# Causal blocks with carried sums of k^T v, transposes on VectorE and double PSUM banks in a retention-plus-SwiGLU kernel

## The chip, the core and the metric

One core of a Trainium2 chip runs the whole program. The metric is the device time of one execution in microseconds, as the median of the runs. The TensorE clock has two levels, 1.2 and 2.4 GHz; the profile gives the granted clock as a share of 2.4 GHz.

## The reference

Retention attention without softmax over 8 sequences of 576 tokens and 8 heads of 64, then RMS norm and a SwiGLU block over the 4608 tokens. All is float32, but the three weight matrices arrive as float64.

```python
scores = scale * np.matmul(q, k.transpose(0, 1, 3, 2))
Dmat = np.where(rel >= 0, gamma[:, None, None] ** rel[None, :, :], 0.0)   # rel = query - key
x = np.matmul(scores * Dmat, v)            # then (B,H,S,D) -> (B*S, H*D)
xn = x / np.sqrt(np.mean(x * x, axis=-1, keepdims=True) + 1e-06) * rms_g
g = xn @ w_gate
out = (g * (1.0 / (1.0 + np.exp(-g))) * (xn @ w_val)) @ w_out
```

## The kernel before

Two streams of work share TensorE. A **job** of attention is one sequence and one pair of heads, 32 jobs in all, and its result is one 128-row chunk of x, transposed (features on the partitions, tokens on the free axis). A **unit** of the FFN is 384 tokens, 12 units in all, and up to four units of x are on chip.

A job: `load` brings q, k and v of both heads by DMA on SP's queue. `turn` transposes q and k with TensorE (tiles tp_q and tp_k, three products of 96 tokens each) and ScalarE copies them out of PSUM as qT and kT. `scores` takes one tile of 128 keys and one block of queries: two products (s, one for each head, in the upper and lower 64 rows of the array), and VectorE multiplies each by a table of decays, which also holds the causal zeros, into ret. Every pair of key tile and block of queries that isn't wholly in the future is computed. `values` multiplies ret by v (the heads side by side in 64 columns of the array each) and sums over the key tiles in PSUM (av); ScalarE copies the sum to x. `attention_step` issues the scores of one tile, then the values of the tile before it, so s and av take turns on TensorE.

When a unit of x is whole, `norm_1` squares it on ScalarE (sq), sums over the features with 12 products of one column (ms), takes the power -1/2 on GpSimd (r) and puts it on diagonals; `norm_2` spreads it over the partitions with one product (rb), and VectorE scales x. Then `gate` and `value` (12 column blocks each, four products of 384 columns per block), Silu on ScalarE, the product h on VectorE, and `contract` (three times 12 products of 512 columns).

The order is written by hand. The loop at the end of the program gives TensorE a step of attention, or a step of the FFN when the FFN's columns fall behind attention's share (it starts 17% behind), or when attention would need a fifth unit of x.

The weights come as float64 in 36 chunks of 128 x 512. `round_chunk` turns one into float32 with six VectorE instructions and one of ScalarE; `weights_to` rounds up to a chunk number and asks for later loads on ScalarE's queue. After the first 8 steps of attention one chunk is rounded with every second step, and `gate` and `contract` round what they need and a little more. PSUM is three pools of single banks: 3 for s, 2 for tp and av, 3 for the FFN.

A float32 product shows in the profile as two records for TensorE and two for its weight loads.

Of the kernel before, what the change touches and what calls it, by code (L numbers as in the profile page):

```python
# [17 lines left out]
def _decay_table(H, S, D):  # L18
    """T[p, h, c] = gamma_h ** (c - p) / sqrt(D) where c >= p, else 0: a key tile that begins at
    token t uses column q - t for query q."""  # L20
    gamma = 1.0 - 2.0 ** (-5.0 - np.arange(H, dtype=np.float64))
    rel = np.arange(S)[None, :] - np.arange(P)[:, None]
    t = np.where(rel >= 0, gamma[:, None, None] ** np.maximum(rel, 0)[None], 0.0) / np.sqrt(D)
    return np.ascontiguousarray(t.transpose(1, 0, 2)).astype(np.float32)


@with_exitstack
def kernel(
# [15 lines left out]
    NHP = H // 2  # head pairs, which are also the 128-row chunks of d_model  # L44
    NF = DFF // P
    NKT = -(-S // P)  # key tiles; the last one is short
    JT = 6  # token tiles of a loaded q or k
    PT = S // JT
# [4 lines left out]
    assert (D, DM, NHP * P) == (64, H * D, DM) and S % JT == 0 and NTOK % U == 0  # L53
# [8 lines left out]
    ps_s = ctx.enter_context(tc.tile_pool(name="ps_s", bufs=3, space=PS))  # L62
    ps_m = ctx.enter_context(tc.tile_pool(name="ps_m", bufs=2, space=PS))
    ps_f = ctx.enter_context(tc.tile_pool(name="ps_f", bufs=3, space=PS))
# [6 lines left out]
    decay = const.tile([P, H, S], F32, name="decay")  # L71
# [10 lines left out]

    def load(j):
        b, hp = jobs[j]
        hs = slice(2 * hp, 2 * hp + 2)
        for nm, src in (("q", q), ("k", k)):
            t = raw.tile([PT, JT, 2, D], F32, tag=nm + "raw", name=f"{nm}raw_{j}")
            for e in range(2):
                nc.sync.dma_start(
                    out=t[:, :, e], in_=src[b, 2 * hp + e].rearrange("(j p) d -> p j d", p=PT)  # L90
                )
            st[j][nm + "raw"] = t
        t = raw.tile([P, 2, NKT, D], F32, tag="v", name=f"v_{j}", bufs=3)
        full = S // P
        for e in range(2):
            nc.sync.dma_start(
                out=t[:, e, :full],
                in_=v[b, 2 * hp + e, : full * P].rearrange("(c p) d -> p c d", p=P),
            )
        if S % P:  # L100
            nc.sync.dma_start(
                out=t[: S % P, :, full], in_=v[b, hs, full * P :].rearrange("h p d -> p h d")
            )
        st[j]["v"] = t

    def turn(j, nm):
        """q or k of a head pair with (head, d) on the partitions."""
        d = st[j]
        t = att.tile([P, S], F32, tag=nm + "T", name=f"{nm}T_{j}")
        tv = t.rearrange("p (j t) -> p j t", j=JT)  # L110
        half = JT // 2
        for n in range(2):
            tp = ps_m.tile([P, half, PT], F32, tag="m", name=f"tp_{nm}_{j}_{n}")
            for i in range(half):
                nc.tensor.transpose(  # L115
                    out=tp[:, i], in_=d[nm + "raw"][:, n * half + i], identity=ident[:PT, :PT]
                )
            nc.scalar.copy(out=tv[:, n * half : (n + 1) * half], in_=tp)  # L118
        d[nm + "T"] = t

    def blocks(b):
        """The queries of a sequence, cut where the FFN's units are."""
        cuts = [0] + [c - b * S for c in range(0, NTOK, U) if 0 < c - b * S < S] + [S]
        return list(zip(cuts[:-1], cuts[1:]))

    def tiles(j):
        return [
            (j, q0, q1, kt)
            for q0, q1 in blocks(jobs[j][0])
            for kt in range(NKT)  # L130
            if kt * P < q1
        ]

    def scores(j, q0, q1, kt):
# [3 lines left out]
        k0, k1 = kt * P, min(kt * P + P, S)  # L138
        lo, n = max(q0, k0), k1 - k0
        w = q1 - lo  # L140
        ret = att.tile([P, 2, U], F32, tag="ret", name=f"ret_{j}_{q0}_{kt}", bufs=3)
        ss = [ps_s.tile([P, 512], F32, tag="s", name=f"s_{j}_{q0}_{kt}_{e}") for e in range(2)]
        for e in range(2):
            r = slice(e * D, e * D + D)
            nc.tensor.matmul(  # L145
                ss[e][:n, :w], lhsT=d["kT"][r, k0:k1], rhs=d["qT"][r, lo:q1], start=True, stop=True
            )
        for e in range(2):
            nc.vector.tensor_tensor(  # L149
                out=ret[:n, e, :w], in0=ss[e][:n, :w],  # L150
                in1=decay[:n, 2 * hp + e, lo - k0 : q1 - k0], op=ALU.mult,
            )
        d["ret", q0, kt] = ret
# [127 lines left out]
    def attention_step(n, t):  # L281
# [4 lines left out]
        if j + 1 < len(jobs):  # L286
            if n == 2:
                turn(j + 1, "q")
# [145 lines left out]
```

## Time and profile before

| | us |
|---|---|
| median of 3 runs (1737.16 to 1738.85) | 1737.68 |
| span of the profiled execution, first to last instruction | 1732.1 |
| TensorE busy | 1609.2 |
| VectorE busy | 387.0 |
| ScalarE busy | 213.7 |
| GpSimd busy | 10.9 |
| mean granted clock, share of 2.4 GHz | 0.917 |

The profile of the execution gives its span; an execution's own time contains what lies around the span too, and for the median that is 5.6 us. Busy time is the union of an engine's records, and a busy TensorE need not be at its peak: records overlap, and at half the clock the same product is busy twice as long. A stretch is read with the granted clock beside it.

### The profile page before, as it was taken

What the parts mean: (1) busy time and instruction counts of PE and PEld (TensorE: products, weight loads), DVE (VectorE), ACT (ScalarE), POOL (GpSimd) and SP (SyncE); (2) the same over time, 40 slices, a digit from 0 to 9 for tenths busy, and PEclk for the clock granted to TensorE, in tenths of its full rate; (3) what the DMA queues carried; (4) which work ended last, traced back from release to release, by engine and by line L of the source; (5) the groups of instructions that cost most, each with busy time, mean ns of one, the idle gap of its engine ahead of it and who ended that gap; (6) DMA issues with size and microseconds to landing.
All of it is one profiled execution on the core that took longest, in us unless ns stands there. A gap on an engine that the chain in (4) does not pass through costs nothing.

```text
span 1732.1 us, 14109 instructions
## 1 busy us (share of the span) xinstructions
PE 1609.2 (93%) x5784; PEld 842.0 (49%) x5784; DVE 387.0 (22%) x940; ACT 213.7 (12%) x422; POOL 10.9 (1%) x18
## 2 busy tenths in 40 slices
PE   5778976999999999999999899999999899999899
PEld 2334532554454554554554554454554554455454
DVE  2655375121111111211111211310111310410110
ACT  1112121110011110110110100110110100200000
POOL 0000000000000000000000000000000000000000
PEclk9556976999998999998999899899899899989899
DMA  6333232100100100100000101200101200100000
GB/s 180 100 88 89 60 113 80 27 14 13 33 14 20 31 17 20 47 0 20 26 21 19 41 1 28 59 0 13 27 7 32 56 1 0 46 1 6 12 0 18
DMA packets 134927, 59.89 MB, mean 35 GB/s; under 512 B 115920, under 2 KB 128208, under 8 KB 134864
## 3 DMA queue, kind: packets, MB, share of 16 engines
q1 hardware_dynamic: 119360, 37.77, 8.7%
q10 hardware_dynamic: 15504, 21.24, 3.9%
q8 instruction: 45, 0.74, 0.2%
q14 instruction: 18, 0.15, 0.0%
HBM read 49.55 MB, written 9.44 MB: 34 GB/s over the span
## 4 chain that ended last, share of the span: by engine, by line
PE 88%; DVE 6%; ACT 4%; issue 1%; DMA 1%; POOLq 0%; SPq 0%; ACTq 0%; DVEq 0%
PE gate L218 23%; PE out L241 22%; PE val L218 22%; PE s L145 8%; PE av L165 7%; PE ms L188 3%; PE tp_k L115 2%; PE tp_q L115 1%; ACT exp L338 1%; DVE exp L342 1%; ACT sq L185 1%; ACT kT L118 1%; PE rb L206 1%; DVE exp L339 1%; ACT x L173 1%
## 5 line engine op out<-in xcount | busy, mean ns | idle before, releaser
L241 PE MATMUL out<-w_out,h 128*128 128x512 f32 x864 | 402.8, 619 | 23.4 <-DVE w_out L352 23.4
L218 PE MATMUL gate<-x,w_gate 128*128 128x384 f32 x1152 | 411.9, 502 | 5.8 <-DVE x L210 5.8
L218 PE MATMUL val<-x,w_val 128*128 128x384 f32 x1152 | 397.8, 488 | 0.0
L218 PEld LDWEIGHTS gate<-x,w_gate 128*128 128x128 f32 x1152 | 221.7, 195 | 168.3 <-issue 15.9
L218 PEld LDWEIGHTS val<-x,w_val 128*128 128x128 f32 x1152 | 216.6, 190 | 151.4 <-issue 5.8
L241 PEld LDWEIGHTS out<-w_out,h 128*128 128x128 f32 x864 | 165.3, 197 | 232.6 <-issue 191.2
L149 DVE TENSOR_TENSOR ret<-s,decay 128x384 f32<-128x384 f32 (+4 forms) x480 | 160.2, 374 | 527.3 <-PE s L145 526.0
L233 DVE TENSOR_TENSOR h<-silu,val 128x384 f32<-128x384 f32 x144 | 79.8, 554 | 612.4 <-PE val L218 612.1
L145 PE MATMUL s<-qT,kT 64*128 64x384 f32 (+4 forms) x960 | 189.9, 433 | 23.5 <-DVE ret L149 23.3
L145 PEld LDWEIGHTS s<-qT,kT 64*128 64x128 f32 (+1 forms) x960 | 88.2, 198 | 146.9 <-issue 109.5
L228 ACT ACTIVATE silu<-gate 128x384 f32<-128x384 f32 x144 | 70.7, 491 | 697.7 <-PE gate L218 686.7
L165 PE MATMUL av<-ret,v 128*64 128x384 f32 (+4 forms) x960 | 156.2, 407 | 0.0
L165 PEld LDWEIGHTS av<-ret,v 128*64 128x64 f32 (+1 forms) x960 | 51.3, 146 | 74.9 <-issue 61.1
L188 PE MATMUL ms<-mean_w,sq 128*128 128x1 f32 x288 | 55.5, 325 | 26.9 <-ACT sq L185 26.9
L188 PEld LDWEIGHTS ms<-mean_w,sq 128*128 128x128 f32 x288 | 54.4, 293 | 29.1 <-ACT sq L185 29.1
L247 ACT COPY o<-out 128x512 f32<-128x512 f32 x36 | 21.1, 586 | 341.7 <-PE out L241 341.7
L115 PE MATMUL tp_k<-ident,kraw 96*128 96x96 f32 x192 | 33.5, 291 | 19.4 <-ACT kT L118 15.5
L115 PE MATMUL tp_q<-ident,qraw 96*128 96x96 f32 x192 | 32.6, 291 | 18.3 <-DMA qraw<-in_q_dram 9.7
L173 ACT COPY x<-av 128x384 f32<-128x384 f32 (+1 forms) x64 | 25.5, 399 | 177.4 <-PE av L165 153.4
L118 ACT COPY kT<-tp_k 128x288 f32<-128x288 f32 x64 | 25.5, 399 | 129.0 <-PE tp_k L115 128.9
L115 PEld LDWEIGHTS tp_k<-ident,kraw 96*128 96x128 f32 x192 | 20.5, 156 | 41.4 <-ACT kT L118 21.9
L115 PEld LDWEIGHTS tp_q<-ident,qraw 96*128 96x128 f32 x192 | 21.1, 160 | 32.1 <-issue 15.7
(33 smaller groups left out, 261.4 us busy)
## 6 DMA issues: line engine op xcount, KB each, us to landing
qraw<-in_q_dram SPq DMA_DIRECT2D x64, 144.0 KB, 2.5
kraw<-in_k_dram SPq DMA_DIRECT2D x64, 144.0 KB, 2.5
out_dram<-o SPq DMA_DIRECT2D x36, 256.0 KB, 2.1
v<-in_v_dram SPq DMA_DIRECT2D x64, 128.0 KB, 2.5
w<-in_moe_w_gate_dram ACTq DMA_DIRECT2D x12, 512.0 KB, 3.4
w<-in_moe_w_val_dram ACTq DMA_DIRECT2D x12, 512.0 KB, 3.6
w<-in_moe_w_out_dram ACTq DMA_DIRECT2D x12, 512.0 KB, 3.4
decay<-decay_table ACTq DMA_DIRECT2D x4, 576.0 KB, 6.3
```

What stands on the lines that cost most here:

```text
L115: nc.tensor.transpose(out=tp[:, i], in_=d[nm + "raw"][:, n * half + i], identity=ident[:PT, :PT])
L118: nc.scalar.copy(out=tv[:, n * half : (n + 1) * half], in_=tp)
L145: nc.tensor.matmul(ss[e][:n, :w], lhsT=d["kT"][r, k0:k1], rhs=d["qT"][r, lo:q1], start=True, stop=True)
L149: nc.vector.tensor_tensor(out=ret[:n, e, :w], in0=ss[e][:n, :w], in1=decay[:n, 2 * hp + e, lo - k0 : q1 - k0], op=ALU.mult,)
L165: nc.tensor.matmul(av[e * D : e * D + D, lo - q0 : q1 - q0], lhsT=d["v"][:n, e, kt], rhs=ret[:n, e, : q1 - lo], start=(kt == 0), stop=last,)
L173: nc.scalar.copy(out=x_of[u][:, hp, c0 : c0 + q1 - q0], in_=av[:, : q1 - q0])
L188: nc.tensor.matmul(ms[:, s : s + 1], lhsT=sq[:, c, s * P : s * P + P], rhs=mean_w, start=(c == 0), stop=(c == NHP - 1),)
L218: nc.tensor.matmul(ps[:, :U], lhsT=w[:, c, f * P : f * P + P], rhs=x_of[u][:, c], start=(c == 0), stop=(c == NHP - 1),)
L228: nc.scalar.activation(out=hs[f], in_=ps[:, :U], func=AF.Silu)
L233: nc.vector.tensor_tensor(out=h, in0=hs[f], in1=ps[:, :U], op=ALU.mult)
L241: nc.tensor.matmul(ps[s][:, :DM], lhsT=hs[f][:, s * P : s * P + P], rhs=w_out[:, f], start=(f == 0), stop=(f == NF - 1),)
L247: nc.scalar.copy(out=o, in_=ps[s][:, :DM])
```

## The change

The causal decay gamma^(query - key) is split in two factors. q is multiplied by gamma^query / 8 and v by gamma^(-key), both on GpSimd. With that the future of a chunk of 128 queries needs no decay table: inside the chunk the scores are masked with ones and zeros, and all earlier chunks enter through one 64 x 64 matrix for each head, the running sum of k^T v.

A job now is 5 chunks (the last of 64 tokens). `scores` computes only the five blocks on the diagonal, `states` the four products k^T v, `weigh` masks the scores with three VectorE instructions and sums the states with four, and GpSimd copies them into a block-diagonal tile sd. `values` multiplies the masked scores by v, and `carried` adds sd times q. q and k come by 8 DMAs of 32 partitions, in pieces of 32 floats laid out so that a VectorE transpose of 32 x 32 blocks gives qT and kT; k comes a second time, untransposed (kn). The square, the sum and the spreading of the norm are three calls (norm_0, norm_1, norm_2), made some steps apart; norm_0 adds the four chunks on VectorE first, so that ms has 3 products in place of 12. PSUM is one pool of four double banks for all tiles. One weight chunk is rounded with every step of attention, and a step is now a whole job.

```diff
+    psum = ctx.enter_context(tc.tile_pool(name="psum", bufs=4, space=PS))
+    def banks(name):
+        return psum.tile([P, 2, 512], F32, tag="ps", name=name)
...
     def load(j):
+            t = raw.tile([P, S // SQ, SQ], F32, tag=nm + "raw", name=f"{nm}raw_{j}")
             for e in range(2):
+                rows = src[b, 2 * hp + e].rearrange("(t b) (i a) -> i b t a", b=SQ, a=SQ)
+                for i in range(D // SQ):
+                    r = e * D + i * SQ
+                    nc.sync.dma_start(out=t[r : r + SQ], in_=rows[i])
+        t = raw.tile([P, NFULL, 2, D], F32, tag="kn", name=f"kn_{j}", bufs=3)
...
+    def prepare(j):
+        for nm, bufs in (("q", 3), ("k", 2)):
+            t = att.tile([P, S], F32, tag=nm + "T", name=f"{nm}T_{j}", bufs=bufs)
+            nc.vector.transpose(out=t, in_=d.pop(nm + "raw").rearrange("p t a -> p (t a)"))
+        nc.gpsimd.tensor_tensor(out=d["qT"], in0=d["qT"], in1=gq[:, hp], op=ALU.mult)
+        for n, cs in ((P, slice(0, NFULL)), (TAIL, slice(NFULL, NC))):
+            t = d["v"][:n, cs]
+            nc.gpsimd.tensor_tensor(
+                out=t, in0=t,
+                in1=gv[:n, hp, cs].unsqueeze(3).to_broadcast([n, cs.stop - cs.start, 2, D]),
+                op=ALU.mult,
...
+    def scores(j):
+        d["s"] = [banks(f"s_{j}_{i}") for i in range(2)]
+        for c in range(NC):
+            for e in range(2):
+                nc.tensor.matmul(
+                    d["s"][blk][:n, e, o : o + n], lhsT=d["kT"][r, ck], rhs=d["qT"][r, ck],
+    def states(j):
+        for c in range(NFULL):
+            for e in range(2):
+                nc.tensor.matmul(
+                    d["s"][1][e * D : e * D + D, 0, SC + c * D : SC + c * D + D],
+                    lhsT=d["kn"][:, c, e], rhs=d["v"][:, c, e], start=True, stop=True,
+    def weigh(j):
+        for blk, c0, c1 in ((0, 0, AC), (1, AC, NFULL), (1, NFULL, NC)):
+            nc.vector.tensor_tensor(
+                out=ret[:n, :, c0 * P : c0 * P + m * n].rearrange("p e (c k) -> p e c k", c=m),
+                in0=s[blk][:n, :, o : o + m * n].rearrange("p e (c k) -> p e c k", c=m),
+                in1=causal[:n, :n].unsqueeze(1).unsqueeze(1).to_broadcast([n, 2, m, n]),
...
+        nc.vector.tensor_copy(out=t[:, 0], in_=part[:, 0])
+        for c in range(1, NFULL):
+            nc.vector.tensor_tensor(out=t[:, c], in0=part[:, c], in1=t[:, c - 1], op=ALU.add)
+        for e in range(2):
+            nc.gpsimd.tensor_copy(out=sd[j % 2][r, :, r], in_=t[r])
...
+    def carried(j):
+        for c in range(1, NC):
+            nc.tensor.matmul(
+                av[:, blk, o : o + n], lhsT=sd[j % 2][:, c - 1], rhs=d["qT"][:, c * P : c * P + n],
...
+        if hp == NHP - 1:
+            for u in range(len(ready) + len(turning), ((b + 1) * S) // U):
+                turning.append([u, 0, norm_0(u), 0])
...
+    def norm_0(u):
+        sq = ffn.tile([P, NHP, U], F32, tag="sq", name=f"sq_{u}", bufs=1)
         nc.scalar.activation(out=sq, in_=x, func=AF.Square)
+        while n > 1:
+            n //= 2
+            nc.vector.tensor_tensor(
+                out=sq[:, :n], in0=sq[:, :n], in1=sq[:, n : 2 * n], op=ALU.add
+            )
...
+    def attention_step(j):
+        if j < len(jobs):
+            scores(j)
+            states(j)
+        if j > 0:
+            values(j - 1)
+        if j < len(jobs):
+            weigh(j)
+        if j > 0:
+            carried(j - 1)
+        if j + 2 < len(jobs):
+            prepare(j + 2)
+        if j + 3 < len(jobs):
+            load(j + 3)
...
-                if did_a > 8 and did_a % 2:
-                    weights_to(n_chunks + 1)
+                weights_to(n_chunks + 1)
+                turned(2)
```

`turned(n)` counts 1 for a step of the FFN and 2 for one of attention and makes the next call of a waiting norm when it has counted 3.

TensorE in the attention, before: the key tiles of one block of queries in a job, s (scores) and av (values) in turn.

```order
L145 MATMUL s_384_2_0_706<-qT_457,kT_498 128x192
L145 MATMUL s_384_2_1_707<-qT_457,kT_498 128x192
L165 MATMUL av_384_665<-ret_384_1_658,v_238 64x192 x2
L145 MATMUL s_384_3_0_715<-qT_457,kT_498 128x192
L145 MATMUL s_384_3_1_716<-qT_457,kT_498 128x192
L165 MATMUL av_384_665<-ret_384_2_705,v_238 64x192 x2
```

And now, one whole step: the scores and states of a job (tiles s_0 and s_1), then the values and the carried part of the job before it (tile av).

```order
L171 MATMUL s_0_324<-qT_206,kT_208 128x128 x6
L171 MATMUL s_1_325<-qT_206,kT_208 128x128 x2
L171 MATMUL s_1_325<-qT_206,kT_208 64x64 x2
L181 MATMUL s_1_325<-v_171,kn_168 64x64 x8
L215 MATMUL av_344<-ret_271,v_131 64x128 x8
L215 MATMUL av_344<-ret_271,v_131 64x64 x2
L228 MATMUL av_344<-qT_151,sd_85 128x128 x3
L228 MATMUL av_344<-qT_151,sd_85 128x64
```

A job was 30 products on average and 12 transposes, with s and av in turn; it is 32 products in four runs. Eight such steps stand ahead of the first gate, and the other 25 stand singly or in runs of 4 or 5 between units: 8 to 11, 12, 13, 14, 15 to 19, 20 to 23, 24 to 27, 28 to 31, and 32, which has only values and carried.

VectorE at the first unit's gates, before: h is the product of silu and value, exp and w are the rounding of a chunk (here number 17 of 36).

```order
L233 TENSOR_TENSOR h_0_945<-silu_0_917,val_0_940 128x384
L149 TENSOR_TENSOR ret_192_1_954<-s_192_1_0_955,decay 128x384
L149 TENSOR_TENSOR ret_192_1_954<-s_192_1_1_956,decay 128x384
L334 TENSOR_SCALAR exp_964<-w_17_879 128x512
L339 TENSOR_SCALAR exp_964<-exp_964 128x512
```

And now, behind the third block of the first unit, where the chunk is number 8.

```order
L314 TENSOR_TENSOR h_2_878<-silu_2_872,gv_2_867 128x384
L424 TENSOR_SCALAR exp_880<-w_8_750 128x512
L429 TENSOR_SCALAR exp_880<-exp_880 128x512
L432 SCALAR_TENSOR_TENSOR exp_880<-w_8_750,exp_880 128x512
L435 TENSOR_SCALAR w_gate<-w_8_750 128x4x128
L439 SCALAR_TENSOR_TENSOR w_gate<-w_8_750,w_gate 128x4x128
L442 SCALAR_TENSOR_TENSOR w_gate<-w_gate,exp_880 128x4x128
```

So 28 chunks are left to round when the gates have begun, two ahead of each h and the last ten ahead of the first contraction, and no attention stands among them.

VectorE in the step in which a sequence ends that completes two units (units 1 and 2 here): the states' sums, the adds of both squares, then the transposes of a later job.

```order
L202 TENSOR_TENSOR sum_1356<-s_1_1322,sum_1356 128x64 x3
L259 TENSOR_TENSOR sq_1370<-sq_1370 128x768
L259 TENSOR_TENSOR sq_1370<-sq_1370 128x384
L259 TENSOR_TENSOR sq_1374<-sq_1374 128x768
L259 TENSOR_TENSOR sq_1374<-sq_1374 128x384
L143 STREAM_TRANSPOSE qT_1378<-qraw_808 128x576
L143 STREAM_TRANSPOSE kT_1380<-kraw_813 128x576
```

Both squares use one buffer, and ms of the first stands on TensorE behind the whole next step; before, each square had its ms at once behind it.

## Rows read from the trace of the kernel before

**Rows 1.** The page's costliest groups, scores and values: busy us, mean ns, idle before.
```profile
L145 PE MATMUL s<-qT,kT 64*128 64x384 f32 (+4 forms) x960 | 189.9, 433 | 23.5 <-DVE ret L149 23.3
L165 PE MATMUL av<-ret,v 128*64 128x384 f32 (+4 forms) x960 | 156.2, 407 | 0.0
```
**Rows 2.** Windows by stage: length, busy PE, PEld, DVE, ACT, POOL; clock, DMA, GB/s.
```profile
14.00:36.00 22.00, 17.91 (x96) 8.96 (x96) 9.04 (x24) 4.95 (x12) 0.00 (x0) 1.00 0.60 150
...
40.00:154.00 114.00, 86.10 (x312) 42.05 (x310) 68.03 (x158) 20.94 (x40) 0.87 (x1) 0.50 0.35 98
154.00:236.00 82.00, 80.87 (x298) 42.89 (x299) 38.89 (x79) 16.61 (x32) 0.00 (x0) 0.97 0.25 71
236.00:292.00 56.00, 32.64 (x57) 10.18 (x57) 39.58 (x78) 9.88 (x15) 0.00 (x0) 0.57 0.34 107
292.00:1732.00 1440.00, 1387.70 (x5010) 735.44 (x5010) 229.44 (x592) 159.94 (x324) 9.36 (x11) 0.96 0.08 20
```
**Rows 3.** Chain of waits in the last unit: start, us, what.
```profile
1623.27 0.49 ACT x L173
...
1623.79 1.49 ACT sq L185
...
1625.32 3.88 PE ms L188 x24
...
1631.14 1.66 PE rb L206 x2
...
1633.57 4.60 PE gate L218 x8
1638.17 2.58 PE val L218 x8
...
1697.51 30.91 PE out L241 x72
```
**Rows 4.** Timeline of TensorE, full clock, then half: start, us, instruction, count.
```profile
520.86 0.92 PE L145 MATMUL s<-qT,kT 64*128 64x384 f32 x4
...
521.70 0.33 PE L165 MATMUL av<-ret,v 64*64 64x64 f32 x4
...
569.34 0.59 PE L145 MATMUL s<-qT,kT 64*128 64x192 f32 x4
...
569.87 0.55 PE L165 MATMUL av<-ret,v 128*64 128x192 f32 x4
...
570.34 7.13 PE L241 MATMUL out<-w_out,h 128*128 128x512 f32 x16
...
148.52 1.01 PE L145 MATMUL s<-qT,kT 64*128 64x192 f32 x4
149.46 0.48 PE L165 MATMUL av<-ret,v 64*64 64x64 f32 x4
```
**Rows 5.** Timeline of VectorE and TensorE while w_out is rounded, one chunk.
```profile
248.41 0.42 DVE L334 TENSOR_SCALAR exp<-w 128x512 uint32<-128x512 uint32 x1
248.55 2.08 PE L241 MATMUL out<-w_out,h 128*128 128x512 f32 x2 [2.99 <-DVE w_out L352]
...
252.48 0.42 DVE L334 TENSOR_SCALAR exp<-w 128x512 uint32<-128x512 uint32 x1
```
**Rows 6.** Groups by form, VectorE and GpSimd: busy us, mean ns.
```profile
L149 DVE TENSOR_TENSOR ret<-s,decay 128x192 f32<-128x192 f32 x192 | 59.7, 352 | 213.5 <-PE s L145 213.5
L149 DVE TENSOR_TENSOR ret<-s,decay 128x384 f32<-128x384 f32 x96 | 49.3, 552 | 99.1 <-PE s L145 99.1
...
L194 POOL TENSOR_TENSOR r<-r,mhalf 128x3 f32<-128x3 f32 x12 | 10.2, 852 | 1618.8 <-DVE r L193 1618.8
masks.py:199 POOL TENSOR_SCALAR_AFFINE_SELECT ident<-ident 128x128 f32<-128x128 f32 x1 | 0.3, 294 | 0.1
```
**Rows 7.** SP's queue: issue of two DMAs, and all its packets.
```profile
0.74 0.95 SPq L89 DMA_DIRECT2D qraw<-in_q_dram  x2
...
q1 hardware_dynamic: 119360, 37.77, 8.7%
```

More of the change, by code (lines that the diff above doesn't have):

```diff
@@ L70 @@
     least = const.tile([P, 1], F32, name="least")
-    decay = const.tile([P, H, S], F32, name="decay")
+    causal = const.tile([P, P], F32, name="causal")
+    gq = const.tile([P, NHP, S], F32, name="gq")
+    gv = const.tile([P, NHP, NC, 2], F32, name="gv")
+    sd = [const.tile([P, NFULL, P], F32, name=f"sd{i}") for i in range(2)]
     rms_g = const.tile([P, NHP], F32, name="rms_g")
@@ L100, in load @@
-        if S % P:
+                out=t[:, :, e],
+                in_=k[b, 2 * hp + e, : NFULL * P].rearrange("(c p) d -> p c d", p=P),
+            )
+        d["kn"] = t
+        t = raw.tile([P, NC, 2, D], F32, tag="v", name=f"v_{j}", bufs=4)
+        for e in range(2):
             nc.sync.dma_start(
-                out=t[: S % P, :, full], in_=v[b, hs, full * P :].rearrange("h p d -> p h d")
-            )
[L104 to L134, printed above, removed]
+                out=t[:, :NFULL, e],
+                in_=v[b, 2 * hp + e, : NFULL * P].rearrange("(c p) d -> p c d", p=P),
+            )
@@ L143, in scores @@
         for e in range(2):
             r = slice(e * D, e * D + D)
[L145 to L153, printed above, removed]
-    def values(j, q0, q1, kt):
+            nc.gpsimd.tensor_copy(out=sd[j % 2][r, :, r], in_=t[r])
@@ new lines, in weigh, with values @@
+        d["ret"] = ret
+    def values(j):
+        d = st[j]
+        av = d["av"] = banks(f"av_{j}")
+        for c in range(NC):
+            n, (blk, o) = rows_of(c), place(c)
+            for e in range(2):
+                nc.tensor.matmul(
+                    av[e * D : e * D + D, blk, o : o + n], lhsT=d["v"][:n, c, e],
+                    rhs=d["ret"][:n, e, c * P : c * P + n], start=(c in (0, AC)), stop=False,
+                    skip_group_check=True,
+                )
+    def carried(j):
@@ L377 @@
         load_chunk(1)
-        turn(0, "q")
-        turn(0, "k")
+        prepare(0)
+        prepare(1)
         load(2)
-        attn = [(n, t) for j in range(len(jobs)) for n, t in enumerate(tiles(j))]
-        n_attn = len(attn)
+        n_attn = len(jobs) + 1
         ffn_cols = sum(c for u in range(NU) for c, _ in ffn_steps(u))
-        did_a, did_f, unit, steps, waited = 0, 0, 0, None, False
+        did_a, did_f, unit, steps = 0, 0, 0, None
         while did_a < n_attn or unit < NU:
-            if turning and waited:
-                turned()
-            waited = bool(turning)
             if steps is None and unit < len(ready):
@@ L392 @@
             due = did_a == n_attn or (did_a / n_attn - LAG) * ffn_cols > did_f * (1 - LAG)
-            if steps is not None and (due or unit + XBUFS <= upto(attn[did_a][1])):
+            full = unit + XBUFS <= upto(min(did_a, len(jobs) - 1))
+            if steps is not None and (due or full):
                 got = next(steps, None)
```

195 lines of the change are left out of this document (109 added, 86 removed).

## Prediction

> **What bounds the kernel now.** I read the windows by stage first, because the work changes over the span. From 292 us on, TensorE is busy 1387.7 of 1440 us at 0.96 of its clock [rows 2]: there the end is set by what TensorE has to do. Before that it is not. From 40 to 154 us, attention alone with weights being rounded, the clock is at 0.50 and TensorE busy 86 of 114 us; from 236 to 292 us it is busy 33 of 56 at 0.57 [rows 2]. In that stretch two records of a contraction wait 2.99 us for VectorE, and from one chunk's first instruction to the next one's are 4.07 us (248.41 to 252.48) [rows 5]. So VectorE, busy 387 us in all, bounds the opening: each of 36 chunks costs 4.07 us there, ScalarE's part included. Third, the chain of the last unit: an FFN unit is 12 gates and 12 values of 2.58 us and 30.91 us of contraction, 92.8 us at the full clock, and the norm ahead of it holds TensorE from 1623.27 to 1633.57 us, with a first gate of 4.60 in place of 2.58 us behind it [rows 3].
>
> **Price of an attention step on TensorE.** From the scores of 384 columns to the next product are 0.84 us (520.86 to 521.70), of 192 columns 0.53; values of 192 columns take 0.47 (569.87 to 570.34) [rows 4]. The two scores lie 192 columns and 0.31 us apart: 1.63 ns for a column of a pair of heads, and 0.22 us fixed. Values at that rate have 0.155 us fixed. I read the fixed part as the first weight load and the emptying of the array, paid when the shape changes; four records inside a run need not pay it again. Taking 1.65 ns: scores 576 columns of pairs, 0.95, and two shapes (0.22 + 0.155), 1.33 us. States 256 columns and one shape, 0.58. Values 576 columns and two shapes, 1.26. Carried 448 columns, 0.74, a shape of 0.22 and about 0.1 because the last 64 columns are fewer than their weights', 1.05. A step is 4.2 us, for some 10.8 us of scores and values now (189.9 + 156.2 over 32 jobs [rows 1], part of it at half clock) and the transposes besides. In the last unit 8 records of 384 columns follow each other every 0.32 us [rows 3], 0.84 ns a column, which is the rate of the columns alone: loads are hidden beneath whole-array products. The Trainium skill ("TensorE: Matmul & The Clock Gate", Part 3, The mechanism) lets a weight load run beneath products only where it goes to another group of rows; those gates speak against it, and what it would make of the sum is rival C.
>
> **The sum, stage by stage, for the changed program.**
>
> *To the first gate, 91 us.* Eight steps stand ahead of it, since the norm's three calls need two steps each. VectorE has per step: the masks of 768, 256 and 128 columns, 0.95 + 0.42 + 0.29 (0.15 us and 1.04 ns a column, from the forms of 192 and 384 [rows 6]); four sums of 64 columns at 0.22, 0.89; two transposes of 576 columns, for which no row exists: 0.47 at the rate of the rounding's one-input form (0.42 for 512 [rows 5]), 0.75 at that of the masks, 1.5 at half that; I take the middle one, 0.75, because nothing in a block transpose resembles the short chain of the first; and one chunk, 4.07. That is 8.1 us; I take 9, as the chunk's ScalarE part stands behind the copies of x, which wait for carried. GpSimd has q (576 columns), v (512 and 128) and two copies of 256 per step. At VectorE's rates these are 2.6 us; at 0.85 fixed, as the power has for three columns, and 2.3 ns a column, as the select has [rows 6], 8.2. The select's 0.29 us for 128 columns is what VectorE would need, so I take 3.5: hidden on its queue. SP issues 13 DMAs a job at 0.48 us [rows 7], 6.2 us, also under 9. Two jobs' loads and transposes come before the first mask: 26 issues, 2.5 us for landing and 1.5: 16 us. 16 + 72 + 3 for the norm's last part is 91; bounds 84 (8.1 a step) and 112 (GpSimd's 3.5 locked against VectorE).
>
> *The first unit, 160 us.* Only 8 chunks are rounded by then, where before 17 were. The first three blocks need none: 18.5 us with a first gate at half clock. Then VectorE has 28 chunks at 4.07 and nine h at 0.55 [rows 6], 119 us, against 46 us of gates at full clock and 10 of contraction: it bounds, as it did at 236 to 292. One product and two contractions follow, 22 us. Bounds 155 and 175 (gates at 1.2 GHz, 10.3 us a block against 8.7).
>
> *Units 1 to 11:* 11 x 92.8 = 1021 us, with Silu, h and output copies beneath them as in the last unit. Double banks leave a gate the bank of four requests ago, over 15 us old.
>
> *Attention:* 24 steps at 4.2 and values and carried alone, 2.3: 103 us; up to 165 by the third rival.
>
> *Norms:* ten units with ms of 6 records at 0.16, rb 0.8 (1.66 at half clock [rows 3]) and the wait for x: 2.3 us each, 23. What goes is 18 ms records and the wait for the square; what is late instead: rb still stands next to its first gate. Unit 10 has nothing to hide behind: the chain of 10.3 us, less 2.9 of ms, and 1.5 of adds, with 2 for the slow gate: 11.
>
> *A new wait:* where a sequence completes two units, both squares share one buffer. The second square waits for ms of the first, which stands behind the next whole step on TensorE; its adds hold VectorE's queue, and behind them stand the transposes of the job after. TensorE, done with ms, waits for square 1.5, adds 0.95 + 0.55, transposes 1.5 and GpSimd's q, about 1: 6 us, and 3 more at half clock after it. Steps 8 to 11, 15 to 19 and 24 to 27 have it: 27 us.
>
> *Rest:* shape changes at the ends of the runs 3, the end from 1728.4 to 1732.1 as now, 4.
>
> 91 + 160 + 1021 + 103 + 23 + 11 + 27 + 7 = 1443 us of span, against 1732.1; the median stands 5.6 above the profiled span, and I keep that: **1449 us.** What about 0.2% moves cannot be told from no change. For this case alone I give 1415 to 1490, most of it the opening and the waits in runs.
>
> **The rivals.**
>
> *A. Half clock in the runs of steps.* Small products and idle feeders may hold the clock at 1.2 GHz as from 40 to 154 us (TensorE busy 0.76 of it); against it, from 14 to 36 us attention alone, busy 0.81, had 1.00 [rows 2]. At half clock scores of 192 columns took 0.94 us (148.52 to 149.46) for 0.53 [rows 4]: a step becomes 7.4, 24 x 3.2 = 77 more, 1526.
>
> *B. GpSimd feeds too slowly.* At 8.2 us a step, the runs' first two steps are prepared ahead, the 11 others wait 4.0 each, 44; in the opening it locks against VectorE's rounding for 3.5 x 8 = 28: 1521. For it speaks the power's 0.85 us for three columns; against it the select's row. "GPSIMD Engine Reference", 3.1, of the Trainium skill has two-input work at half VectorE's pace, which gives an estimate of some 2.7 us for the three products; no run here shows it. "SBUF — State Buffer", Who interferes with whom, says that a VectorE instruction with two SBUF inputs and a reading GpSimd one exclude each other.
>
> *C. Every weight load stands in line.* Read for 64-row and 64-column shapes, the mechanism is that a record's weights, 128 columns for scores, states half as many, go in only after the record before: the column part doubles in scores, states and carried and grows by half in values, 0.95 + 0.42 + 0.74 + 0.47 = 2.6 us a step, 62 in all: 1511. The rule of "TensorE: Matmul & The Clock Gate" quoted above would do this. Against it: values of 192 columns took 0.47, not the 0.43 of a pure alternation without emptying [rows 4].
>
> *D. Slower than before.* The loads of pieces of 32 floats bound the steps that no FFN hides, 8 in the opening and 11 in the runs. It turns to a loss when each costs 15 us more, that is 19 us a job in a run and 24 in the opening. A load has 4608 such pieces; a packet of this queue now takes 20 ns (8.7% of 16 engines over 119360 packets, 316 bytes on average [rows 7]), so with the other 2176 pieces of a job at 20 ns these would have to take some 74. At exactly that, 1738; I know no row that points there.
>
> **How the numbers follow.** Forecast 0.70, A 0.10, B 0.12, C 0.05, D 0.03. The range 1410 to 1540 holds the forecast with its ends, and A, B and C singly; two of them together and D are left out. Faster 0.96, the same 0.01, slower 0.03.
>
> **What would show it.** First gate at about 91 us and the end of the first unit near 250, with VectorE as what TensorE waits for in between; a step of 4.2 us in a run, by scores, states, values and carried as above; some 6 us of TensorE idle behind ms in three runs, ended by GpSimd's q or VectorE's transposes; the clock at 1.00 from 250 us on except there. If runs of steps take over 6 us a step, one of A, B and C holds, told apart by the clock, by the engine waited for, and by the spacing of records. A first unit done by 220 us, or no wait for the second square, would prove me wrong in the sum's two largest guesses.

## The result, and the profile after

The changed kernel takes 1638.44 us (median of 4 runs, 1636.89 to 1640.44), the kernel before 1738.26 (median of 4, 1737.16 to 1743.21). The ratio is 0.9418, with a 95% interval from 0.9403 to 0.9433: faster by 100 us, where 289 had been forecast, and outside the range. The span of the profiled execution is 1638.6 us, 195.6 more than the sum's 1443; the execution itself took 1640.4, so 1.8 lie around the span. Every execution with its own span on record has 1.7 to 1.9 around it; the 5.6 must have set the median against the span of another, faster execution.

TensorE's costliest groups, for [rows 1]: busy us, mean ns, and after the second bar the idle time just before and what ended it.

```profile
L297 PE MATMUL gv<-x,w_val 128*128 128x384 f32 x1152 | 427.3, 516 | 134.6 <-ACT silu L307 134.5
L297 PE MATMUL gv<-x,w_gate 128*128 128x384 f32 x1152 | 407.4, 498 | 26.8 <-DVE x L290 26.8
...
L171 PE MATMUL s<-qT,kT 64*128 64x128 f32 (+1 forms) x640 | 57.4, 320 | 66.2 <-DVE ret L192 22.9
L215 PE MATMUL av<-ret,v 128*64 128x128 f32 (+1 forms) x640 | 51.1, 305 | 0.0
L228 PE MATMUL av<-qT,sd 128*128 128x128 f32 (+1 forms) x256 | 37.1, 289 | 0.7 <-POOL sd L205 0.7
...
L181 PE MATMUL s<-v,kn 128*64 128x64 f32 x512 | 27.4, 263 | 0.5 <-POOL v L148 0.4
```

Scores and values kept TensorE busy for 346 us before; scores, values, carried and states now do for 173. That is most of the gain, with the 66 us of TensorE's transposes that went (tp_k 33.5 and tp_q 32.6 before). The first line holds the loss: ahead of the value's products TensorE stands idle for 134.5 us, waiting for Silu. Before the change it waited there for nothing:

```profile
L218 PE MATMUL val<-x,w_val 128*128 128x384 f32 x1152 | 397.8, 488 | 0.0
```

Windows by stage (columns as in [rows 2]; first gate at 108.8 us, first contraction at 254.6, end of the first unit at 320.5):

```profile
109.00:255.00 146.00, 85.17 (x193) 45.30 (x194) 64.73 (x123) 18.88 (x30) 0.00 (x0) 0.76 0.24 73
...
320.00:1639.00 1319.00, 1196.66 (x4558) 655.27 (x4556) 206.71 (x454) 118.35 (x240) 89.00 (x125) 0.98 0.12 26
```

In the gates of the first unit VectorE is busy for 65 of 146 us, so it isn't the bound there that I took it for; and from 320 us on TensorE stands idle for 122 us. A block in the middle of a unit (timeline: start, us, engine and instruction, count, in brackets the idle time before and its releaser):

```profile
1199.37 2.74 PE L297 MATMUL gv<-x,w_gate 128*128 128x384 f32 x8
...
1202.15 0.49 ACT L307 ACTIVATE silu<-gv 128x384 f32<-128x384 f32 x1 [5.52 <-PE gv L297]
...
1202.69 2.85 PE L297 MATMUL gv<-x,w_val 128*128 128x384 f32 x8 [0.58 <-ACT silu L307]
...
1205.38 2.74 PE L297 MATMUL gv<-x,w_gate 128*128 128x384 f32 x8
```

Gate and value are now the halves of one tile (`gate` allocates `gv`, `value` writes `ps[:, 1]`). The value's first product waits for Silu, which reads the other half. From gate to gate are 6.01 us in place of two times 2.58, 0.85 more: 0.58 idle; 0.16 because the gate's products run out with nothing behind them (2.74 to their end, where the next ones would begin at 2.58); and 0.11 because the value's begin on an empty engine (2.69 from their start to the next gate). A unit without attention or norms in it lasts 103.2 us (813.1 to 916.3). In the first unit the same wait becomes a loop:

```profile
138.43 0.49 ACT L307 ACTIVATE silu<-gv 128x384 f32<-128x384 f32 x1 [3.07 <-DVE w_val L442]
138.98 5.49 PE L297 MATMUL gv<-x,w_val 128*128 128x384 f32 x8 [6.86 <-ACT silu L307]
...
144.57 0.56 DVE L314 TENSOR_TENSOR h<-silu,gv 128x384 f32<-128x384 f32 x1 [6.24 <-PE gv L297]
...
152.57 0.38 ACTq L410 DMA_DIRECT2D w<-in_moe_w_val_dram  x1
...
153.05 0.49 ACT L307 ACTIVATE silu<-gv 128x384 f32<-128x384 f32 x1 [2.76 <-DVE w_val L439]
```

Silu stands on ScalarE's queue behind its part of the rounding of the next two chunks, these stand on VectorE behind h of the block before, h waits for the value, and the value now waits for Silu. What ends Silu's wait in eight of the nine blocks that round is the chunk's last read (L439): on ScalarE's queue, between its Relu and Silu, stands the issue of a later weight load (L410), which waits until VectorE has read the chunk whose place it takes. While two chunks are rounded TensorE stands for 6.9 us, and while TensorE runs a value, at half clock (0.50 from 138.98 to 143.6), VectorE stands for 6.2. From h to h are 14.2 us here and 13.7 in the last blocks, where 8.7 had been forecast.

An attention step, and the third step of the run from 320 us on:

```profile
320.47 1.42 PE L171 MATMUL s<-qT,kT 64*128 64x128 f32 x20
321.82 0.69 PE L181 MATMUL s<-v,kn 128*64 128x64 f32 x16
322.33 1.31 PE L215 MATMUL av<-ret,v 128*64 128x128 f32 x20
323.57 1.10 PE L228 MATMUL av<-qT,sd 128*128 128x128 f32 x8
324.61 1.42 PE L171 MATMUL s<-qT,kT 64*128 64x128 f32 x20
...
328.65 0.78 PE L268 MATMUL ms<-mean_w,sq 128*128 128x1 f32 x6
334.91 2.49 PE L171 MATMUL s<-qT,kT 64*128 64x128 f32 x20 [5.47 <-POOL qT L145]
```

By the starts, scores take 1.35 us, states 0.51, values 1.24, carried 1.04: 4.14, where the sum had 1.33, 0.58, 1.26 and 1.05, together 4.2. The wait behind ms is there, ended by GpSimd's q as forecast.

### The profile page after: what moved, and what is told of

It reads as the page before. It is cut to its first block, busy times and chain, and to the rows that moved or that the text cites. A ratio compares the mean times of both kernels' runs of the same rounds, so it can differ in the third digit from the quotient of the medians.

```text
span 1638.6 us, 13258 instructions
## 1 busy us (share of the span) xinstructions
PE 1374.8 (84%) x5312; PEld 758.2 (46%) x5312; DVE 373.8 (23%) x772; ACT 160.4 (10%) x310; POOL 131.2 (8%) x180
## 3 DMA queue, kind: packets, MB, share of 16 engines
q1 hardware_dynamic: 228928, 46.17, 14.0%
## 4 chain that ended last, share of the span: by engine, by line
PE 74%; DVE 11%; ACT 6%; DMA 3%; SPq 3%; issue 2%; POOL 2%; ACTq 0%; DVEq 0%; POOLq 0%
PE gv L297 48%; PE out L322 22%; ACT silu L307 4%; SPq L116 2%; DMA kraw<-in_k_dram 2%; ACT exp L428 2%; DVE exp L432 1%; DVE ret L192 1%; DVE exp L429 1%; DVE exp L424 1%; PE s L171 1%; DVE kT L143 1%; PE av L215 1%; PE av L228 1%; ACT sq L255 1%
## 5 line engine op out<-in xcount | busy, mean ns | idle before, releaser
L297 PE MATMUL gv<-x,w_val 128*128 128x384 f32 x1152 | 427.3, 516 | 134.6 <-ACT silu L307 134.5
L297 PE MATMUL gv<-x,w_gate 128*128 128x384 f32 x1152 | 407.4, 498 | 26.8 <-DVE x L290 26.8
L297 PEld LDWEIGHTS gv<-x,w_val 128*128 128x128 f32 x1152 | 215.4, 197 | 344.5 <-ACT silu L307 221.4
L297 PEld LDWEIGHTS gv<-x,w_gate 128*128 128x128 f32 x1152 | 223.6, 195 | 188.9 <-issue 25.2
L314 DVE TENSOR_TENSOR h<-silu,gv 128x384 f32<-128x384 f32 x144 | 79.8, 554 | 888.6 <-PE gv L297 888.6
L307 ACT ACTIVATE silu<-gv 128x384 f32<-128x384 f32 x144 | 70.7, 491 | 764.5 <-PE gv L297 739.4
L171 PE MATMUL s<-qT,kT 64*128 64x128 f32 (+1 forms) x640 | 57.4, 320 | 66.2 <-DVE ret L192 22.9
L192 DVE TENSOR_TENSOR ret<-s,causal 128x768 f32<-128x768 f32 (+2 forms) x96 | 47.5, 542 | 167.4 <-PE s L171 166.3
L148 POOL TENSOR_TENSOR v<-v,gv 128x512 f32<-128x512 f32 x64 | 49.3, 790 | 29.2 <-DMA v<-in_v_dram 29.2
L215 PE MATMUL av<-ret,v 128*64 128x128 f32 (+1 forms) x640 | 51.1, 305 | 0.0
```

The costliest lines, as they stand in the source:

```text
L148: nc.gpsimd.tensor_tensor(out=t, in0=t, in1=gv[:n, hp, cs].unsqueeze(3).to_broadcast([n, cs.stop - cs.start, 2, D]), op=ALU.mult,)
L171: nc.tensor.matmul(d["s"][blk][:n, e, o : o + n], lhsT=d["kT"][r, ck], rhs=d["qT"][r, ck], start=True, stop=True,)
L192: nc.vector.tensor_tensor(out=ret[:n, :, c0 * P : c0 * P + m * n].rearrange("p e (c k) -> p e c k", c=m), in0=s[blk][:n, :, o : o + m * n] ...
L215: nc.tensor.matmul(av[e * D : e * D + D, blk, o : o + n], lhsT=d["v"][:n, c, e], rhs=d["ret"][:n, e, c * P : c * P + n], start=(c in (0, A ...
L297: nc.tensor.matmul(ps[:, :U], lhsT=w[:, c, f * P : f * P + P], rhs=x_of[u][:, c], start=(c == 0), stop=(c == NHP - 1),)
L307: nc.scalar.activation(out=t, in_=ps[:, 0, :U], func=AF.Silu)
```

## The experiments

Three theories stood against each other for the 134.5 us. Theory 1: the shared tile makes the value wait. Theory 2: Silu itself comes late, since it has two buffers where there were three. Theory 3: four double banks are too few.

**Gate and value in tiles of their own.**

```diff
-        ps = banks(f"gv_{u}_{f}")
-        project(u, f, w_gate, ps[:, 0])
+        ps = banks(f"gate_{u}_{f}")[:, 0]
+        project(u, f, w_gate, ps)
...
-        t, ps = hs[f]
+        t, ps = hs[f], banks(f"val_{u}_{f}")[:, 0]
```

> The changed kernel with one edit: gate and value each take a PSUM tile of their own (one half of a double bank used) in place of the two halves of one tile. Theory 1 (the value's products wait for Silu because both are in one tile: 0.58 us of idle and 0.27 us of refilling for each of 132 blocks behind the first unit, 134.5 us of idle in the trace in all): no wait of a value for Silu is left, a unit without attention goes from 103 to 93 us, so units 1 to 11 give back 0.85 x 132 = 112 us, and the first unit, whose rounding then goes on while the value runs, up to 50 more: 1470 to 1530 us. Theory 2 (Silu itself comes late, behind two buffers where there were three): 1638 within 5. Theory 3 (four double banks are too few): with twice as many tiles in turn the waits grow, 1640 or more.

Measured: 1489.21 us (4 runs), ratio to before 0.8559, interval 0.8535 to 0.8582; span 1480.2. A block of it, and three of TensorE's longest waits (us in total, times, longest):

```profile
1204.70 2.74 PE L297 MATMUL gate<-x,w_gate 128*128 128x384 f32 x8
...
1207.28 2.74 PE L297 MATMUL val<-x,w_val 128*128 128x384 f32 x8
1207.48 0.49 ACT L307 ACTIVATE silu<-gate 128x384 f32<-128x384 f32 x1 [4.67 <-PE gate L297]
1209.86 2.74 PE L297 MATMUL gate<-x,w_gate 128*128 128x384 f32 x8
```

```profile
PE gate L297 <- DVE x L290: 27.6, 7, 14.6
PE out L322 <- DVE w_out L442: 25.8, 12, 2.8
...
PE s L171 <- POOL qT L145: 18.9, 5, 5.5
```

No product waits for Silu, gate to gate is 5.16 us, a unit without attention or norms lasts 93.0 us (725.3 to 818.3), and the first unit lasts from 110.5 to 273.9 us, 163. 149 us of the 189 that I missed are this one wait. That VectorE's rounding bounds the first unit then, as my sum had it, is tested further down.

**The next gate ahead of the value**, with the shared tile kept:

```diff
-            yield NHP * U, lambda f=f: gate(u, f, hs)
+            if f + 1 < NF:
+                yield NHP * U, lambda f=f: gate(u, f + 1, hs)
             yield NHP * U, lambda f=f: value(u, f, hs)
```

(The first block's gate is made ahead of the loop.)

> The changed kernel with gate and value still in one tile, but the next block's gate ahead of the value, so that Silu runs beneath 2.58 us of gate. Theory 1: the value finds Silu done, units 1 to 11 give back the same 112 us; in the first unit two more chunks are rounded ahead of each h, so it gains less than with two tiles: 1500 to 1535 us. Theory 2 (late Silu, buffers): Silu of the next block then waits for an h that comes a value later, 1638 or above. Theory 3 (too few banks): two tiles are in use at once, 1638 or above.

Measured: 1485.75 us (4 runs), ratio 0.8542, 0.8527 to 0.8556. With a gate between, the same wait costs 17.9 us (9 times) in place of 134.5 (139 times). So it is one of the program's order, and two ways lead round it. That the first unit would gain less was wrong: it takes 163.0 us here, and the time lies below the range that was expected.

**Three buffers for Silu.**

```diff
-        t = ffn.tile([P, U], F32, tag="silu", name=f"silu_{u}_{f}", bufs=2)
+        t = ffn.tile([P, U], F32, tag="silu", name=f"silu_{u}_{f}", bufs=3)
```

> The changed kernel with three buffers for Silu's result, as before the change, in place of two. Theory 1 (shared tile): 1638 within 5. Theory 2 (Silu late for want of a buffer): 1520 to 1540, as the 0.85 us of each block go. Theory 3: 1638 within 5.

Measured: 1637.83 us (2 runs). Theory 2 falls; and theory 3 fell with the first run, which takes twice as many tiles in turn.

**The sharing alone, in the kernel before.** The scores get two banks in place of three, the FFN two double banks in place of three banks, and the value is written to the other half of the gate's tile.

```diff
-    ps_s = ctx.enter_context(tc.tile_pool(name="ps_s", bufs=3, space=PS))
+    ps_s = ctx.enter_context(tc.tile_pool(name="ps_s", bufs=2, space=PS))
-    ps_f = ctx.enter_context(tc.tile_pool(name="ps_f", bufs=3, space=PS))
+    ps_f = ctx.enter_context(tc.tile_pool(name="ps_f", bufs=2, space=PS))
...
+        both = ps_f.tile([P, 2, 512], F32, tag="f", name=f"gv_{u}_{f}")
+        ps = project(u, f, w_gate, both[:, 0])
```

> The kernel before the change with this one part of it added: gate and value in the two halves of one double bank (two such tiles for the FFN; the scores have two banks in place of three). Theory 1: each of 144 values waits for Silu unless a step of attention stands between gate and value; at 0.85 us and a step of attention in a third to none of the blocks that is 80 to 122 us more: 1820 to 1860. Theories 2 and 3 put nothing on the sharing itself: 1738 within 15, what the score bank less may cost.

The control has two banks for the scores and four single banks for the FFN, without sharing:

> The control of e4_before_shared (1862.7 us): the kernel before, with its eight banks dealt as there (two for the scores, two for transposes and values, four for the FFN) but gate and value in tiles of their own. If the sharing made that run's 124 us: 1738 within 10. If the third bank of the scores that was taken made them: 1850 or more.

Measured: 1862.71 us (2 runs, ratio 1.0713, 1.0673 to 1.0754) against 1748.03 for the control (8 runs, 1.0053, 1.0035 to 1.0070). The sharing alone costs the kernel before 115 us; the banks dealt otherwise cost 9 of the 124. Of the 115, 79 are TensorE's idle time for Silu, in 112 waits. The value's group of the shared form, then of the control:

```profile
L217 PE MATMUL gv<-x,w_val 128*128 128x384 f32 x1152 | 415.8, 505 | 79.0 <-ACT silu L228 79.0
```

```profile
L218 PE MATMUL val<-x,w_val 128*128 128x384 f32 x1152 | 398.0, 489 | 0.0
```

**The second square behind the first one's ms** (on two tiles, as all that follow):

```diff
-                turning.append([u, 0, norm_0(u), 0])
+                turning.append([u, 0, None if turning else norm_0(u), 0])
...
             turning[0] = [u, 1, norm_1(u, got), 0]
+            if len(turning) > 1:
+                turning[1][2] = norm_0(turning[1][0])
```

> On the kernel with two tiles (e1_two_tiles, 1489.2 us, span 1480.2): where a sequence completes two units, the square of the second and its adds are made behind the first one's ms, in place of ahead of it. Theory 1 (the second square's wait for ms holds VectorE's queue and with it the transposes and GpSimd's q, 5.5 us of idle and a slow clock behind it, three times): 18 to 27 us less, 1462 to 1472. Rival (the wait moves: the second unit's norm is then late for its own first gate, or the run is bound by the loads anyway): 1489 within 6.

Measured: 1475.77 us (4 runs), ratio 0.8484, 0.8463 to 0.8505; 13 less than with two tiles, and less than I expected. TensorE in the first run of steps with two squares:

```profile
280.18 0.78 PE L268 MATMUL ms<-mean_w,sq 128*128 128x1 f32 x6
282.27 1.72 PE L171 MATMUL s<-qT,kT 64*128 64x128 f32 x20 [1.31 <-POOL qT L145]
...
288.86 1.42 PE L171 MATMUL s<-qT,kT 64*128 64x128 f32 x20 [0.84 <-ACT x L239]
...
291.25 1.35 PE L215 MATMUL av<-ret,v 128*64 128x128 f32 x20 [0.36 <-DVE ret L192]
293.59 1.10 PE L228 MATMUL av<-qT,sd 128*128 128x128 f32 x8 [0.98 <-POOL sd L205]
```

The 5.47 us are 1.31, but TensorE now waits further on in the run. The three runs together, from the last contraction to the next gate, are 86.1 us long in place of 91.7. The rest of the 11.7 us by which the two profiled spans differ lies elsewhere: 3.1 us in the chain ahead of unit 10 (11.9 for 15.0), where the second square's adds no longer stand ahead of r, and 3.1 in the opening, which is no more than first gates differ anyway.

Whether those later waits are the square's, moved, can be read from two other runs of steps (20 to 23 and 28 to 31), in which a sequence completes one unit and no second square exists. With two tiles, before this edit:

```profile
828.40 1.42 PE L171 MATMUL s<-qT,kT 64*128 64x128 f32 x20 [1.24 <-POOL qT L145]
...
833.51 1.42 PE L171 MATMUL s<-qT,kT 64*128 64x128 f32 x20 [0.90 <-POOL v L148]
...
838.27 1.10 PE L228 MATMUL av<-qT,sd 128*128 128x128 f32 x8 [0.98 <-POOL sd L205]
...
843.90 4.51 PE L297 MATMUL gate<-x,w_gate 128*128 128x384 f32 x8 [3.82 <-DVE x L290]
```

Much the same waits stand there, so they are not the square's: a run that doesn't wait 5.47 us has them with or without a second square. These two runs last 25.6 and 22.5 us; the three with a second square last 29.0, 29.0 and 29.5 (33.7 less one step). The second square is worth 3 to 7 us a run, 10 to 20 in three, of which the edit gives back 5.6.

**The opening.** With two tiles the first gate stands at 110.5 us, where 91 had been forecast. In four runs: a fourth buffer for kn; long pieces for q and k, which puts their values in other places; GpSimd's products left out, and with them the decay; the last two together.

```diff
-        t = raw.tile([P, NFULL, 2, D], F32, tag="kn", name=f"kn_{j}", bufs=3)
+        t = raw.tile([P, NFULL, 2, D], F32, tag="kn", name=f"kn_{j}", bufs=4)
```

> On the kernel with two tiles: four buffers for the untransposed k in place of three. Theory P (the opening is late because SP's queue stands at the load of kn until the states of three jobs before are done, up to 4.4 us a job, and q and k of the next job stand behind it): the transposes' wait for DMA goes, 21 us of VectorE idle before the first gate to under 8, first gate from 110 to about 97, 1475. Theory Q (the DMA engines themselves are full, 0.8 busy over the opening): first gate within 3 of 110, 1489 within 5.

```diff
-                rows = src[b, 2 * hp + e].rearrange("(t b) (i a) -> i b t a", b=SQ, a=SQ)
+                rows = src[b, 2 * hp + e].rearrange("(i b t) (c a) -> i b (t c) a", i=D // SQ, b=SQ, a=SQ)
```

> On the kernel with two tiles: q and k are loaded with the same eight DMAs and bytes, but each partition takes 576 floats that lie together, so q and k's places are mixed up and the output is another; everything else is the same work. Theory Q (pieces of 32 floats fill the DMA engines in the opening): packets of the q and k loads fall to a tenth or so, VectorE's wait for them goes, first gate from 110 to about 95, 1473. Theory P (SP's order): first gate within 4 of 110, 1489 within 5.

```diff
-        nc.gpsimd.tensor_tensor(out=d["qT"], in0=d["qT"], in1=gq[:, hp], op=ALU.mult)
-        for n, cs in ((P, slice(0, NFULL)), (TAIL, slice(NFULL, NC))):
-            t = d["v"][:n, cs]
-            nc.gpsimd.tensor_tensor(
...
```

> On the kernel with two tiles (1489.2, first gate at 110.5): GpSimd's products of q and v with their tables are left out, so the decay is missing from the output; all else stands. Theory L (while GpSimd multiplies, VectorE's instructions with it are stretched: the eight chunks before the first gate were busy 35.7 us where 3.34 each, 26.7, is the clean time): that stretch goes but for the copies of sd, and the first gate comes 6 to 9 us earlier, 102 to 105; in the runs q's 1.4 us goes from the wait ahead of the third step; 1476 to 1483 in all. Rival (the loads alone pace the opening, and VectorE only waits longer for them): first gate within 3 of 110, 1483 to 1490.

> Both edits of the opening at once, on the kernel with two tiles (first gate at 110.5 us): q and k in long pieces (alone 102.9) and no products on GpSimd (alone 106.3); q and k's places are mixed up and the decay is missing from the output. If loads and stretched VectorE instructions take turns in pacing the opening, each hides part of the other, and both away give more than the two gains added: first gate at 91 to 97, as the sum of VectorE's clean work had it, 1466 to 1472 in all. If the gains only add: 98.7. If something else sets the opening: 102 or more.

| on two tiles | first gate | VectorE's idle time for q and k, from 15 us to it | median |
|---|---|---|---|
| nothing | 110.5 | 20.9 | 1489.2 |
| four kn buffers | 108.6 | 20.8 | 1483.8 (2 runs) |
| long pieces | 102.9 | 10.9 | 1478.4 (2 runs) |
| no products on GpSimd | 106.3 | 25.9 | 1481.0 (2 runs) |
| the last two | 96.9 | 15.7 | 1461.8 (2 runs) |

The idle times are those of the two transposes' groups, here with two tiles:

```profile
L143 DVE STREAM_TRANSPOSE kT<-kraw 128x576 f32<-128x576 f32 x10 | 7.7, 770 | 15.0 <-DMA kraw<-in_k_dram 15.0
L143 DVE STREAM_TRANSPOSE qT<-qraw 128x576 f32<-128x576 f32 x9 | 7.0, 777 | 5.9 <-DMA qraw<-in_q_dram 5.9
```

Theory P falls: with a fourth buffer nothing that kn could wait for is left, and SP still stands several us at kn. The two loads of kn of one job with four buffers, and what ended SP's waits there from 15 to 100 us:

```profile
64.67 5.38 SPq L120 DMA_DIRECT2D kn<-in_k_dram  x2
65.52 0.37 ACTq L410 DMA_DIRECT2D w<-in_moe_w_val_dram  x1
```

```profile
SPq L120 <- DMA w<-in_moe_w_gate_dram: 7.5, 3, 3.8
SPq L120 <- DMA w<-in_moe_w_val_dram: 5.3, 3, 4.5
```

The same with long pieces, where v comes next on SP's queue:

```profile
60.99 0.93 SPq L120 DMA_DIRECT2D kn<-in_k_dram  x2
64.95 1.53 SPq L127 DMA_DIRECT2D v<-in_v_dram  x2
```

```profile
SPq L127 <- DMA w<-in_moe_w_gate_dram: 13.0, 4, 4.4
SPq L127 <- DMA w<-in_moe_w_val_dram: 9.3, 3, 4.2
```

The 5.38 us are two issues of 0.50 and 0.38 and a wait of 4.50 between them, which ends when the weight load that ScalarE asked for at 65.52 has landed. The second kn load needs nothing from that load; in the trace's records both report on the same semaphore. With long pieces the wait is not gone, it stands ahead of v. From 15 to 100 us such waits make 18.5 us with two tiles, 12.8 with four buffers, 14.9 without the products, 22.3 with long pieces and 16.0 with both edits. A weight load is issued when VectorE has read a chunk, and VectorE's next transposes wait for SP's loads: a loop through two queues again. SP is hardly free between its issues and these waits: with two tiles an issue takes 0.54 us, 13 of them 7.0, and from one job's first load to the next one's are 10.9 us (41.4 to 95.8, five jobs), about VectorE's 11.1 from step to step. No run took this wait away, so what it costs isn't shown.

Theory Q holds for some 8 of the 19.5 us: with long pieces SP's queue has 89664 packets in place of 228928, and the first gate comes 7.6 us earlier. Without GpSimd's products the eight chunks' instructions are busy 26.6 us, the clean time, in place of 35.7, but five of the nine us come back as waiting for DMA: the first gate comes 4.2 us earlier. Both edits give 13.6, where the two alone add up to 11.8. First gates of kernels with the same opening lie 3 us apart, so turn-taking and plain addition can't be told apart here. Some 6 us of the 19.5 stay open; VectorE still waits 15.7 us for loads then, and SP 16.0 for weight loads, which no run tests as their cause.

**ScalarE's part of the rounding covered.** The two mantissa instructions are moved between the first instruction and the one that waits for ScalarE.

```diff
         nc.scalar.activation(out=e.bitcast(F32), in_=e, func=AF.Relu, bias=least)
+        nc.vector.tensor_scalar(
+            out=dst.bitcast(U32), in0=hi, scalar1=0xFFFFF, scalar2=0x100000,
...
+            out=dst, in0=lo, scalar=2.0**-32, in1=dst.bitcast(U32), op0=ALU.mult, op1=ALU.add
         nc.vector.tensor_scalar(
             out=e, in0=e.bitcast(F32), scalar1=255.0, scalar2=2.0**23, op0=ALU.min, op1=ALU.mult
```

> On the kernel with two tiles: in the rounding of a chunk VectorE makes the two mantissa instructions while ScalarE makes its one, in place of after it. My sum holds VectorE to be the bound of the first unit at 4.07 us a chunk, 0.8 of them a wait for ScalarE: a chunk then takes 3.3, 28 of them 22 us less, the first unit from 163 to about 141 us, and up to 6 less in the opening: 1461 to 1469. Rival (TensorE at half clock is the bound of the first unit): within 5 of 1489.

Measured: 1456.27 us (2 runs), ratio 0.8367, 0.8342 to 0.8392. The first unit lasts from 103.9 to 243.4 us, 139.5, and the time lies 5 us below the range that was expected: the unit is 24 us shorter, and the first gate is 6.6 earlier, of which some 3 may be the scatter of first gates. From one chunk to the next are 3.21 us:

```profile
129.65 0.42 DVE L424 TENSOR_SCALAR exp<-w 128x512 uint32<-128x512 uint32 x1
...
132.86 0.42 DVE L424 TENSOR_SCALAR exp<-w 128x512 uint32<-128x512 uint32 x1
```

VectorE's rounding does set the first unit, once the Silu wait is gone; the rival falls.

**The edits together**: two tiles, late square, covered Relu.

> Two tiles, late second square and covered Relu together. The three act in different stretches (every block; three runs of steps; the first unit and the opening), so their gains add: 1489 less 13 less 33, 1443 within 6. If they share a cause, 1455 or more.

Measured: 1446.77 us (4 runs), ratio to before 0.8313, 0.8288 to 0.8338. The three gains added would have given 1443; they add to within 4 us. This form beats both kernels.

## Why the prediction was wrong, step by step

**The step that failed** is the one under the units: "Units 1 to 11: 11 x 92.8 = 1021 us, with Silu, h and output copies beneath them as in the last unit. Double banks leave a gate the bank of four requests ago, over 15 us old." I asked how old the bank is that a new tile gets, and didn't ask who else holds the tile that a product writes into. In the last unit before, Silu lay beneath the value because the value had a tile of its own; the diff took that away, and I carried the row over. The wait is the program's: gate and value lie in different banks. The Trainium skill ("PSUM — Partial Sum Buffer", PSUM bank collisions raise a hardware error) has two engines at once in one bank and quadrant (32 partitions) raise an error, and the same pairs on different banks run clean. The trace with two tiles agrees with the second part: Silu reads its bank from 1207.48 while the value is written into another from 1207.28. No run here had Silu and the value at work in one tile at the same time.

**First gate**, forecast 91 (84 to 112): 108.8, near the upper bound, and 110.5 with two tiles. VectorE's own terms held (masks 1.47 us for three, sums 0.95, transposes 0.78 each, for 1.66, 0.89 and 0.75). I had VectorE as the only pace of this stage; its waits for the loads of q and k, some 20 us, and GpSimd's stretching, 9 us of busy time, weren't in the 9 us a step. The term that failed is "SP issues 13 DMAs a job at 0.48 us, 6.2 us, also under 9": with 0.54 an issue, and 2.5 to 4.6 us of waiting for a weight load in five of eight jobs, SP takes 10.9.

**First unit**, forecast 160: 212, and 163 without the Silu wait. The mechanism was right for a program without the shared tile, as the covered Relu shows.

**Attention step**, forecast 4.2, measured 4.14, each part within 0.07 us. That fits the reading of a fixed price for each change of shape; no run varied the shapes to test it.

**Second square**, forecast 27 us for three runs: the wait of 5.5 us is there, in three runs, with a low clock behind it (0.53 from 288.25 to 295.2 with two tiles). But the price was set against runs that wait for nothing. Two plain runs show 1.24 us behind ms as well, and further waits for GpSimd's q, v and sd and for VectorE; against them the second square costs 10 to 20 us in all, and the edit gave back 5.6.

**What is left with two tiles**, 40 us above the forecast: the first gate 19.5, the first unit 3, what follows it 14, and 3 that lie between the median and the span. Of the 14 some 13 are in the five runs of steps, 139.8 us long, for which the sum had 127 (21 steps, five norms and the 27). That the three runs with a second square came within 3 us of the sum (91.7 for 88.5) is luck: one term was too high, and the waits that every run has were put at nothing, as the two plain runs show (48.1 for 38.2).

**Rivals.** A didn't come: the clock is at 0.98 from 320 us on. C didn't come: a step is 4.14 us. B was right in kind for the opening (9 us of stretch for 28); in the runs waits that GpSimd ends exist, but with two tiles, the second square's three apart, they make about 7 us where B had 44. D's mechanism showed in the opening alone, some 8 us: a packet of SP's queue takes 16 ns (with two tiles 15.5% of 16 engines over 228928 packets in 1480.2 us), where D needed 74. No rival had the shared tile, and that one wait is worth 149 us.

**What would show it.** "VectorE as what TensorE waits for" in the first unit was the line to look at: the trace has ScalarE's Silu there.

## What to carry to other kernels

When two results share a tile, list who writes and who reads each half, and in which order: a write into one half stands behind a read of the other wherever nothing lies between them, even in different banks. The cost is small in one block (0.85 us) and is paid in every block; give each result its own tile, or put other work between the read and the write. Where a wait is closed through a second queue (value, h, rounding, Silu), price it as a loop: the engines then take turns, and each one's busy share falls to about half (TensorE 85 and VectorE 65 of 146 us here) while nothing seems to be the bound.

Ask also what ends an issuing engine's wait before blaming the size of its packets: here a load on one queue waited for the landing of a load on another.

## What the chip showed that I had not expected

While GpSimd multiplies, VectorE's instructions on SBUF can be stretched by 0.85 us. The same instruction twice in the opening of the changed kernel, clean and stretched:

```profile
51.25 0.69 DVE L432 SCALAR_TENSOR_TENSOR exp<-w,exp 128x512 uint32<-128x512 uint32 x1
...
63.01 1.85 POOL L148 TENSOR_TENSOR v<-v,gv 128x512 f32<-128x512 f32 x2 [2.11 <-DMA v<-in_v_dram]
63.07 1.54 DVE L432 SCALAR_TENSOR_TENSOR exp<-w,exp 128x512 uint32<-128x512 uint32 x1
```

The Trainium skill ("SBUF — State Buffer", Who interferes with whom) says that a VectorE instruction with two SBUF inputs and a reading GpSimd one exclude each other; the trace agrees for the one shown. One-input instructions of the rounding are stretched too (L435 with two tiles: 0.42 us alone, 1.27 at 86.32 beneath a product of v). Leaving the products out takes the stretch away (35.7 to 26.6 us over eight chunks).

A load on SP's queue stood up to 4.5 us until a weight load from ScalarE's queue had landed, though it needs no byte of it, in the opening of the changed kernel (15.8 us in all from 15 to 100 us) and of every run listed in the table (12.8 to 22.3).
